# A grouped attention kernel whose Q rows stand in another order in three of eight chunks, and whose output is stored in an 8 by 8 pattern

## The chip, the cores and the metric

The kernel runs on one core of one Trainium2 chip. The metric is the device time in microseconds. Three runs of the kernel before took 341.83, 343.13 and 343.47 us; their median, 343.13 us, is the time before. Durations inside the kernel come from one profiled execution.

The core has five engines with a queue of instructions each: PE (TensorE, the matmuls), DVE (VectorE), ACT (ScalarE), POOL (GpSimd) and SP (SyncE, which here only issues DMAs). Sixteen DMA engines move the data between the memory of the chip and SBUF.

## The reference, cut to what matters

```python
B, Hq, Hkv, Sq, Sk, D = 16, 32, 8, 16, 2048, 128      # q, k, v in bfloat16
k = jnp.repeat(k, 4, axis=1); v = jnp.repeat(v, 4, axis=1)
scores = einsum("bhqd,bhkd->bhqk", q, k) * D ** -0.5
out = einsum("bhqk,bhkd->bhqd", softmax(scores, axis=-1), v)
```

Four query heads of 16 rows share one head of K and V. So each of the 16 x 8 = 128 K/V heads meets 64 rows of Q, which lie behind one another in memory. K and V are 67 MB each, Q and the output 2.1 MB each.

## The kernel before, in words

**Units.** A *pair* p (0 to 63) is two K/V heads, and so 128 rows of Q and of the output: the first 64 partitions belong to one head and the last 64 to the other. K is loaded for two pairs at once (32 loads of 2 MB, `Kn`, three slots), V for one pair (64 loads of 1 MB, `Vb`, seven slots; the last is cut into two DMAs), Q for a *chunk* of eight pairs (8 loads of 256 KB, `Qn`, two slots), and the output is stored pair by pair (64 stores of 32 KB from eight buffers `Osb`, 128 rows of 256 B each).

**Q.** A chunk c has 1024 rows. Its load (`load_q`) puts eight rows that follow one another into each partition: row 8a + j lies in partition a at place j. POOL (DVE for chunk 0) makes four masked copies in `Q4` (`lay_q`, L174). PE transposes them by matmuls with the identity (L278), four 128x128 tiles into one PSUM bank of 512 columns (a *stage*), and ACT evicts each stage to `QT` (L404). There are four such evictions in a chunk. In PSUM the columns stand as (j, a); the eviction turns them into (a, x, j), which is the order of the rows in memory: in steps over j, four elements at a time, it reads with a stride of 128 elements and writes 4 elements in a row. Columns of `QT` are the weights of the score matmuls, so their order is the order of the rows of scores, and of the partitions of the output.

**One pair.** DVE transposes K (two STREAM_TRANSPOSE for each score step, `kt`, L351). PE computes scores (L300 and L256). DVE takes them from PSUM, scaled and with the row's extreme (L373). ACT computes exp with the row sum (L413). PE transposes the weights (L312), ACT evicts them (L423), PE multiplies with V (PV, L330 for most pairs, L336 for each fourth and the last eight), and ACT divides by the row sum into `Osb` (norm, L436 and L440; for the last five pairs DVE does it, L394).

**Order.** The programs of PE and ACT are written out beforehand (`pe_prog`, `act_prog`): scores run two pairs ahead, PV four pairs behind (`PVLAG`), and the four parts of the next chunk's Q follow the pairs 2 to 5 of a chunk.

**SP's queue.** SP goes through steps t. In a step it issues, in this order: a Q load where t = 8c - 7; for even t the K load t/2, after a wait for its slot (L208); the V load of pair t - 6, after a wait for its slot (L216); and the store of pair t - 14, after a wait for its norm (L236). All DMAs go through one queue. At the end SP waits until all stores have landed. Before a buffer `Osb[p % 8]` is written again, ACT or DVE waits for the store of pair p - 8 by the count of its semaphore, which grows by 16 with each store.

Of the kernel before, what the change touches and what calls it, by code (L numbers as in the profile page):

```python
# [5 lines left out]
ACT = mybir.ActivationFunctionType  # L6
# [10 lines left out]
NO = 8  # L17
# [6 lines left out]
LASTV = ((0, 12), (12, 16))  # L24
NFAST = 8
NLATE = 5


def both_heads(p, NP):
# [3 lines left out]
def bass_standalone__gqa_softmax__sampling_kernel(  # L33
# [11 lines left out]
    NP = G // 2  # L45
# [21 lines left out]
    QT = [sb(f"QT{i}", [128, 2, 1024], F32) for i in range(2)]  # L67
# [28 lines left out]
    sem_ev = sem("sem_ev")  # L96
# [61 lines left out]
    last_q = {what[1:]: u for u, what in enumerate(stages) if what[0] == "Q"}  # L158
    last_p = {what[1:]: u for u, what in enumerate(stages) if what[0] == "P"}

    def stage_ap(u):
        return ST_ps[:, 512 * (u % NSTAGE):512 * (u % NSTAGE + 1)]

# [15 lines left out]
    with nc.Block() as block:  # L179
# [22 lines left out]
        @block.sync  # L202
        def _(sp):
            def load_k(n):
                s = n % NK
                if n >= NK:
                    sp.wait_ge(sem_kt, 4 * (n - NK) + 4)
                sp.dma_start(Kn[s][:, :], kf[n]).then_inc(sem_k[s], 16)  # L208

            def load_v(p):  # L210
                s = p % NV
                if p >= NV:
                    sp.wait_ge(sem_pv, p - NV + 1)
                if p < NP - 1:
                    dst = Vb[s][:, :, :, :].rearrange("a g j d -> a g (j d)")
                    sp.dma_start(dst, vf[:, 2 * p:2 * p + 2, :]).then_inc(sem_v[s], 16)  # L216
                    return
                for x, (lo, hi) in enumerate(LASTV):
                    dst = Vb[s][:, :, lo:hi, :].rearrange("a g j d -> a g (j d)")
                    src = vf[:, 2 * p:2 * p + 2, 128 * lo:128 * hi]  # L220
                    sp.dma_start(dst, src).then_inc(sem_vl[x], 16)

            def load_q(c):
                s = c % NQ
                if c >= NQ:
                    sp.wait_ge(sem_q4, 4 * (c - NQ + 1))
                src = qf[1024 * c:1024 * (c + 1), :].rearrange("(a j) d -> a j d", j=8)
                sp.dma_start(Qn[s][:, :, :], src).then_inc(sem_q[s], 16)

            def store(p):  # L230
                s = p % NO
                if p < NP - NLATE:
                    sp.wait_ge(sem_nm, p + 1)
                else:
                    sp.wait_ge(sem_nl, p - (NP - NLATE) + 1)
                sp.dma_start(of[128 * p:128 * (p + 1), :], Osb[s][:, :]).then_inc(sem_o[s], 16)  # L236

            for t in range(NP + SLAG + 1):
                for c in range(NQC):
                    if t == max(0, 8 * c - QLEAD):  # L240
                        load_q(c)
                if t < NP and t % 2 == 0:
                    load_k(t // 2)
                if 0 <= t - VLAG < NP:
                    load_v(t - VLAG)
                if 0 <= t - SLAG < NP:
                    store(t - SLAG)
            for s in range(NO):
                sp.wait_ge(sem_o[s], 16 * (NP // NO))

        @block.tensor
        def _(pe):
# [92 lines left out]
        @block.vector  # L345
        def _(dve):
            def kt(n, e):
                Q, x = divmod(n, 2)
                if x == 0:
                    dve.wait_ge(sem_k[Q % NK], 16 * (Q // NK + 1))  # L350
                dve.transpose(  # L351
                    KT[n % NKT][:, :].rearrange("p (t b g e a) -> p e g t b a", t=J // 4, b=2, g=4, e=2)[:, e],
                    Kn[Q % NK][:, :].bitcast(F32).rearrange(
                        "p (g x t e b c) -> p x e g t b c", g=4, x=2, e=2, b=2, c=32)[:, x, e],
                ).then_inc(sem_kt, 1)

            def recip(Q):
                dve.wait_ge(sem_exp, 2 * Q + 2)
                dve.reciprocal(rrec[:, 2 * Q:2 * Q + 2], rowsum[:, 2 * Q:2 * Q + 2]).then_inc(sem_rec, 1)  # L359

            dve.wait_ge(sem_id, 8)
            lay_q(dve, 0)
            for n in range(2):
                for e in range(2):
                    kt(n, e)
            for n in range(NP):
                Q, x = divmod(n, 2)
                dve.wait_ge(sem_s, n + 1)
                for y in range(2):
                    p = 2 * Q + y  # L370
                    if x == 0 and p >= NS:
                        dve.wait_ge(sem_exp, p - NS + 1)
                    dve.tensor_scalar(  # L373
                        Sneg[p % NS][:, 1024 * x:1024 * (x + 1)].rearrange("p (t a m) -> p t a m", t=4, m=8),
                        S_ps[:, 1024 * y:1024 * (y + 1)].rearrange("p (t m a) -> p t a m", t=4, m=8), -scale, None,
                        op0=ALU.mult, op1=ALU.min, accum_out=nhalf[:, x, p:p + 1],
                    ).then_inc(sem_max, 1)
                if x == 1:
                    dve.wait_ge(sem_max, 2 * n + 2)
                    pair = slice(2 * Q, 2 * Q + 2)  # L380
                    dve.tensor_tensor(nbias[:, pair], nhalf[:, 0, pair], nhalf[:, 1, pair], op=ALU.min).then_inc(sem_nb, 1)  # L381
                elif n >= 4:
                    recip(Q - 2)
                if n + 2 < NP:
                    for e in range(2):
                        kt(n + 2, e)
            recip(NQD - 2)
            for p in range(NP - NLATE, NP):
                if p == NP - 2:
                    recip(NQD - 1)  # L390
                dve.wait_ge(sem_rec, p // 2 + 1)
                dve.wait_ge(sem_o[p % NO], 16 * (p // NO))
                dve.wait_ge(sem_pv, p + 1)
                dve.tensor_scalar(Osb[p % NO][:, :], o_ap(p), rrec[:, p:p + 1], None, op0=ALU.mult).then_inc(sem_nl, 1)  # L394

        @block.scalar
        def _(act):
            for op in act_prog:
                if op[0] == "qe":
                    _, c, i, u = op  # L400
                    act.wait_ge(sem_st, u + 1)
                    if c >= 2 and i == 0:
                        act.wait_ge(sem_s, 8 * (c - 1))
                    act.activation(  # L404
                        QT[c % 2][:, i // 2, :].rearrange("p (a x j) -> p x a j", x=2, j=4)[:, i % 2],
                        stage_ap(u).rearrange("p (j a) -> p a j", j=4), ACT.Copy,
                    ).then_inc(sem_ev, 1)
                elif op[0] == "exp":
                    _, p = op
                    act.wait_ge(sem_nb, p // 2 + 1)  # L410
                    if p >= 2:
                        act.wait_ge(sem_st, last_p[p - 2, 1] + 1)
                    act.activation(  # L413
                        P[p % 2][:, :].bitcast(BF16),
                        Sneg[p % NS][:, :], ACT.Exp,
                        bias=nbias[:, p:p + 1], scale=-1.0, accum_out=rowsum[:, p:p + 1],
                    ).then_inc(sem_exp, 1)
                elif op[0] == "pe":
                    _, p, h, u = op
                    act.wait_ge(sem_st, u + 1)  # L420
                    if h == 0 and p >= NPT:
                        act.wait_ge(sem_pv, p - NPT + 1)
                    act.activation(  # L423
                        PT[p % NPT][:, 4 * h:4 * (h + 1), :].rearrange("p t q -> p (t q)"),
                        stage_ap(u), ACT.Copy,
                    ).then_inc(sem_ev, 1)
                else:
                    _, p = op
                    act.wait_ge(sem_pv, p + 1)
                    act.wait_ge(sem_rec, p // 2 + 1)  # L430
                    if p >= NO:
                        act.wait_ge(sem_o[p % NO], 16 * (p // NO))
                    if both_heads(p, NP):
                        for g in range(2):
                            rows = slice(64 * g, 64 * (g + 1))
                            ins = act.activation(Osb[p % NO][rows, :], O_ps[rows, 128 * g:128 * (g + 1)], ACT.Copy,  # L436
                                                 scale=rrec[rows, p:p + 1])
                        ins.then_inc(sem_nm, 1)
                        continue
                    act.activation(Osb[p % NO][:, :], o_ap(p), ACT.Copy,  # L440
                                   scale=rrec[:, p:p + 1]).then_inc(sem_nm, 1)
# [28 lines left out]
```

## Time and profile before

| what | value |
| --- | --- |
| median of three runs | 343.13 us (341.83 to 343.47) |
| span of the profiled execution | 340.7 us |
| PE busy, matmuls | 304.3 us (89%) |
| DVE busy | 304.8 us (89%) |
| ACT busy | 253.6 us (74%) |
| POOL busy | 81.3 us (24%) |
| moved by DMA | 138.87 MB, mean 408 GB/s |
| median time from issue to landing | K 15.3, V 16.6, Q 13.3, stores 16.1 us |

The page of the profile gives the span, from the first to the last instruction, and no other time of that execution. The difference to the runs (2.4 us to their median) holds what lies around the span and what executions differ by.

How to read the lines that follow: a group's line names the line of the code, the engine, the operation, what it writes and reads, the number of instructions, the busy time, the mean of one in ns, and the idle time before it with what ended it. In the rows of 40 slices a digit is the busy share of a slice in tenths. In a timeline, the first number is the start and the second the duration in us; a DMA issue on SP is as long as SP was held by it.

### The profile page before, as it was taken

The numbers are of one execution on the slowest core, as the hardware profiler recorded it, in microseconds if no ns is written. First come the engines' busy times: TensorE is split into PE (matmuls) and PEld (weight loads), VectorE is DVE, ScalarE is ACT, GpSimd is POOL, SyncE is SP. The second block draws the span as 40 slices with busy tenths as digits, with TensorE's granted clock in tenths as the row PEclk, the third lists the DMA queues.
The fourth block names the chain that finished last, engine by engine and source line by source line (L and its number), as shares of the span: only waits on it lengthen the run. The fifth ranks groups of instructions, "written<-read, shape, count | busy, mean of one in ns | idle before, by whom it ended". The sixth has DMA issues, their size and how long they took to land.

```text
span 340.7 us, 7084 instructions
## 1 busy us (share of the span) xinstructions
PE 304.3 (89%) x3040; PEld 182.4 (54%) x2528; DVE 304.8 (89%) x457; ACT 253.6 (74%) x390; POOL 81.3 (24%) x40
## 2 busy tenths in 40 slices
PE   3466798999899998999989999999989999899987
PEld 3012355555655664566555556556645665555556
DVE  1879998999989997999989999899979999899952
ACT  3025776789777888778867897778887788678875
POOL 2840007500092004900075000920039000000000
PEclk9759999999999999999999999999999999999999
DMA  7999999999999999999999999999999999999993
GB/s 294 443 415 420 425 415 414 411 419 422 424 423 410 415 419 424 416 420 407 419 426 423 419 405 417 421 428 415 412 418 416 426 418 423 408 419 415 410 407 121
DMA packets 32688, 138.87 MB, mean 408 GB/s; under 512 B 10896, under 2 KB 11152, under 8 KB 28560
## 3 DMA queue, kind: packets, MB, share of 16 engines
q1 hardware_dynamic: 32656, 138.42, 99.5%
q8 instruction: 22, 0.36, 0.4%
q14 instruction: 10, 0.08, 0.1%
HBM read 136.31 MB, written 2.10 MB: 406 GB/s over the span
## 4 chain that ended last, share of the span: by engine, by line
PE 55%; DVE 28%; ACT 9%; issue 5%; DMA 2%; ACTq 0%; SPq 0%; DVEq 0%
PE O_ps L330 17%; DVE Sneg L373 17%; PE S_ps L300 14%; PE S_ps L256 12%; DVE KT L351 11%; PE ST_ps L312 8%; ACT P L413 4%; ACT QT L404 2%; DMA Kn<-in_k_dram 2%; PE ST_ps L278 2%; ACT PT L423 2%; ACT O L436 1%; PE S_ps L336 1%; PE O_ps L336 1%; DVE rrec L359 0%
## 5 line engine op out<-in xcount | busy, mean ns | idle before, releaser
L373 DVE TENSOR_SCALAR_CACHE_REDUCE Sneg<-S_ps 128x1024 f32<-128x1024 f32 x128 | 150.7, 1213 | 19.1 <-PE S_ps L256 18.9
L351 DVE STREAM_TRANSPOSE KT<-Kn 128x1024 f32<-128x1024 f32 x128 | 150.8, 1217 | 3.9 <-DMA Kn<-in_k_dram 3.9
L413 ACT ACTIVATE P<-Sneg,nbias 128x2048 bf16<-128x2048 f32 x64 | 128.2, 2004 | 16.1 <-DVE nbias L381 15.1
L300 PE MATMUL S_ps<-KT,QT 64*128 64x512 bf16 x512 | 103.5, 394 | 24.1 <-DVE Sneg L373 12.8
L174 POOL TENSOR_SCALAR Q<-Qn,mask 128x1024 bf16<-128x1024 bf16 x28 | 79.1, 2843 | 181.1 <-PE ST_ps L278 174.6
L256 PE MATMUL S_ps<-KT,QT 64*128 64x512 bf16 x512 | 103.1, 392 | 0.0
L330 PEld LDWEIGHTS O_ps<-Vb,PT 128*128 128x128 bf16 x672 | 62.4, 98 | 34.7 <-issue 28.0
L330 PE MATMUL O_ps<-Vb,PT 128*128 128x256 bf16 x672 | 80.7, 273 | 0.0
L423 ACT ACTIVATE PT<-ST_ps 128x512 f32<-128x512 f32 x128 | 69.3, 595 | 13.1 <-PE ST_ps L312 12.1
L300 PEld LDWEIGHTS S_ps<-KT,QT 64*128 64x128 bf16 x512 | 27.4, 94 | 93.7 <-issue 72.4
L312 PE MATMUL ST_ps<-ident,P 128*128 128x128 f32 x512 | 67.6, 275 | 4.1 <-ACT P L413 4.1
L436 ACT ACTIVATE O<-O_ps,rrec 64x128 bf16<-64x128 f32 x84 | 30.4, 362 | 46.2 <-PE O_ps L330 45.7
L312 PEld LDWEIGHTS ST_ps<-ident,P 128*128 128x128 f32 x512 | 56.9, 141 | 10.3 <-ACT P L413 7.8
L278 PE MATMUL ST_ps<-ident,Q 128*128 128x128 f32 x128 | 20.4, 291 | 5.2 <-DVE Q L174 5.2
L404 ACT ACTIVATE QT<-ST_ps 128x512 f32<-128x512 f32 x32 | 19.3, 604 | 5.1 <-PE ST_ps L278 5.1
L336 PEld LDWEIGHTS O_ps<-Vb,PT 128*64 128x64 bf16 x576 | 16.7, 110 | 11.5 <-issue 11.5
L336 PE MATMUL O_ps<-Vb,PT 128*64 128x128 bf16 x576 | 19.5, 221 | 0.6 <-ACT O L440 0.6
L278 PEld LDWEIGHTS ST_ps<-ident,Q 128*128 128x128 f32 x128 | 16.4, 152 | 5.2 <-issue 5.2
L413 ACT ACTIVATION_READ_ACCUMULATOR P<-Sneg,nbias 128x1 f32 x64 | 12.2, 191 | 0.0
L373 DVE DVE_READ_ACCUMULATOR Sneg<-S_ps 128x1 f32 x128 | 10.6, 83 | 0.0
L440 ACT ACTIVATE O<-O_ps,rrec 128x128 bf16<-128x128 f32 x17 | 6.0, 351 | 2.2 <-PE O_ps L336 2.2
L381 DVE TENSOR_TENSOR nbias<-nhalf 128x2 f32<-128x2 f32 x32 | 5.1, 160 | 1.1
(19 smaller groups left out, 20.1 us busy)
## 6 DMA issues: line engine op xcount, KB each, us to landing
Kn<-in_k_dram SPq DMA_DIRECT2D x32, 2048.0 KB, 15.3
Vb<-in_v_dram SPq DMA_DIRECT2D x63, 1024.0 KB, 16.6
Qn<-in_q_dram SPq DMA_DIRECT2D x8, 256.0 KB, 13.3
out_dram<-O SPq DMA_DIRECT2D x64, 32.0 KB, 16.1
Vb<-in_v_dram SPq DMA_DIRECT2D x1, 768.0 KB, 12.0
Vb<-in_v_dram SPq DMA_DIRECT2D x1, 256.0 KB, 12.3
```

Source lines behind the costliest of these rows:

```text
L174: eng.tensor_scalar(Q4[:, :, :, r, :].rearrange("p j b x -> p (j b) x"), src, mask[:, r:r + 1], None, op0=ALU.mult,).then_inc(sem_q4, 1)
L256: return pe.add_instruction(mybir.InstMatmult(name=nc.get_next_instruction_name(), engine=mybir.EngineType.PE, ins=[pe.lower_ap(rhs), pe.l ...
L278: ins = pe.transpose(dst[:, 128 * j:128 * (j + 1)], src[:, 4 * x + j, b, :], ident4[:, :])
L300: ins = pe.matmul(s_ap, w, x, start=(acc == 0), stop=(acc == 3))
L312: ins = pe.transpose(dst[:, 128 * t:128 * (t + 1)], P[p % 2][:, 128 * x:128 * (x + 1)], ident4[:, :])
L330: ins = pe.matmul(O_ps[:, 0:256], pt[:, j // 2, j % 2, :], Vb[p % NV][:, :, j, :], start=(j == 0), stop=(j == J - 1),)
L336: ins = pe.matmul(o_ap(p)[64 * g:64 * (g + 1), :], pt[:, j // 2, j % 2, 64 * g:64 * (g + 1)], Vb[p % NV][:, g, j, :], start=(j == 0), stop ...
L351: dve.transpose(KT[n % NKT][:, :].rearrange("p (t b g e a) -> p e g t b a", t=J // 4, b=2, g=4, e=2)[:, e], Kn[Q % NK][:, :].bitcast(F32). ...
L373: dve.tensor_scalar(Sneg[p % NS][:, 1024 * x:1024 * (x + 1)].rearrange("p (t a m) -> p t a m", t=4, m=8), S_ps[:, 1024 * y:1024 * (y + 1)] ...
L413: act.activation(P[p % 2][:, :].bitcast(BF16), Sneg[p % NS][:, :], ACT.Exp, bias=nbias[:, p:p + 1], scale=-1.0, accum_out=rowsum[:, p:p + ...
L423: act.activation(PT[p % NPT][:, 4 * h:4 * (h + 1), :].rearrange("p t q -> p (t q)"), stage_ap(u), ACT.Copy,).then_inc(sem_ev, 1)
L436: ins = act.activation(Osb[p % NO][rows, :], O_ps[rows, 128 * g:128 * (g + 1)], ACT.Copy, scale=rrec[rows, p:p + 1])
```

## The change

`TURNED = (1, 3, 5)` names three chunks, 24 of the 64 pairs. In these chunks

- the eviction of Q writes the 64 rows of a head in the order (x, j, a) in place of (a, x, j): the row 8a + j of a head comes to the place 8j + a, in steps of eight rows. It reads eight neighbouring elements of PSUM at a time and writes 32 in a row.
- the rows of scores, of the weights and of O stand in that order too. Nothing else in the computation changes.
- a store is two DMAs, one for each half of 64 partitions, and the rows of the output are named by a pattern j, a: partition 8j + a goes to row 8a + j. Each adds 16 to the semaphore, 32 for the pair, and the waits for a buffer count accordingly (`stored`).

```diff
+TURNED = (1, 3, 5)
...
+    def stored(p):
+        return sum(32 if x // 8 in TURNED else 16 for x in range(p % NO, p + 1, NO))
...
-                sp.dma_start(of[128 * p:128 * (p + 1), :], Osb[s][:, :]).then_inc(sem_o[s], 16)
+                if p // 8 not in TURNED:
+                    sp.dma_start(of[128 * p:128 * (p + 1), :], Osb[s][:, :]).then_inc(sem_o[s], 16)
+                    return
+                for g in range(2):
+                    rows = of[128 * p + 64 * g:128 * p + 64 * (g + 1), :].rearrange("(a j) d -> j a d", j=8)
+                    sp.dma_start(rows, Osb[s][64 * g:64 * (g + 1), :]).then_inc(sem_o[s], 16)
...
-                dve.wait_ge(sem_o[p % NO], 16 * (p // NO))
+                dve.wait_ge(sem_o[p % NO], stored(p - NO))
...
-                    act.activation(
-                        QT[c % 2][:, i // 2, :].rearrange("p (a x j) -> p x a j", x=2, j=4)[:, i % 2],
-                        stage_ap(u).rearrange("p (j a) -> p a j", j=4), ACT.Copy,
-                    ).then_inc(sem_ev, 1)
+                    if c in TURNED:
+                        to = QT[c % 2][:, i // 2, :].rearrange("p (h x j a) -> p x h j a", x=2, j=4, a=8)[:, i % 2]
+                        turned = stage_ap(u).rearrange("p (j h a) -> p h j a", j=4, a=8)
+                    else:
+                        to = QT[c % 2][:, i // 2, :].rearrange("p (a x j) -> p x a j", x=2, j=4)[:, i % 2]
+                        turned = stage_ap(u).rearrange("p (j a) -> p a j", j=4)
+                    act.activation(to, turned, ACT.Copy).then_inc(sem_ev, 1)
```

The waits of ACT before a norm and of SP at the end are changed in the same way.

More of the change, by code (lines that the diff above doesn't have):

```diff
@@ L248, in _ @@
             for s in range(NO):
-                sp.wait_ge(sem_o[s], 16 * (NP // NO))
+                sp.wait_ge(sem_o[s], stored(NP - NO + s))
         @block.tensor
@@ L431, in _ @@
                     if p >= NO:
-                        act.wait_ge(sem_o[p % NO], 16 * (p // NO))
+                        act.wait_ge(sem_o[p % NO], stored(p - NO))
                     if both_heads(p, NP):
```

## The prediction

> **What bounds the kernel now.** I read the page first, then the instructions of the K loads, the queue of SP in order of time, and the end of PE.
>
> ```profile
> span 340.7 us, 7084 instructions
> ...
> DMA  7999999999999999999999999999999999999993
> DMA packets 32688, 138.87 MB, mean 408 GB/s; under 512 B 10896, under 2 KB 11152, under 8 KB 28560
> q1 hardware_dynamic: 32656, 138.42, 99.5%
> PE 55%; DVE 28%; ACT 9%; issue 5%; DMA 2%; ACTq 0%; SPq 0%; DVEq 0%
> L404 ACT ACTIVATE QT<-ST_ps 128x512 f32<-128x512 f32 x32 | 19.3, 604 | 5.1 <-PE ST_ps L278 5.1
> ```
>
> By the chain, PE and DVE set the end and the DMA has 2%. But the DMA engines are busy from the first slice to the last but one. Both are true: the loads arrive just in time. The next lines show how just. First the last K load in the view of its tile (window 295 to 297), then the DVE timeline at the transpose that reads it:
>
> ```profile
> L208 SPq DMA_DIRECT2D Kn<-in_k_dram x1: 1220/1220/1220, 295.8 to 295.8; - x1
> DMA to landing us min/median/max: 19.9/19.9/19.9
> ```
>
> ```profile
> 316.24 1.22 DVE L351 STREAM_TRANSPOSE KT<-Kn 128x1024 f32<-128x1024 f32 x1
> ```
>
> Issued at 295.76 us, landed 19.9 us later: 315.6. DVE came to it at 316.24. The spare time is 0.6 us. The same subtraction for earlier K loads gives 4.2 us (K25, wanted at 257.67), 2.6 (K27), 1.1 (K28), 2.3 (K29), 1.6 (K30): the loads fall behind, about 10.1 us for two pairs of heads where compute takes 9.4 to 10. V of the last pair lands at 336.0 and 336.8 us (issued 324.02 and 324.45, 12.0 and 12.3 us to landing), and PE reaches it at about 337.3 and 338.1: 1.3 us. The queue of SP shows the same from the other side:
>
> ```profile
> 186.04 0.47 SPq L236 DMA_DIRECT2D out_dram<-O  x1
> ...
> 297.51 6.55 SPq L236 DMA_DIRECT2D out_dram<-O  x1
> ```
>
> The same store takes 0.47 us to issue, and 6.55 us late in the run, where the queue is full and SP waits for room. So the kernel is bound by compute with 0.6 us to spare, and whatever the engines of the DMA have to do beyond that comes out at the end.
>
> One thing more, from the trace's records of the landings: each DMA lands in sixteen parts, one for each engine (169 DMAs, 169 x 16 = 2704 parts; with 64 x 128 = 8192 packets of store rows that makes the page's 10896 under 512 B). Early on the sixteen parts land within 0.6 us. At the end they do not: of the last V, six land between 331.9 and 332.8 us, four between 334.7 and 335.1, six between 335.6 and 336.8. Ten engines have been set back, by the fetches of instructions (22 packets of 16 KB, about 1.05 us each; late parts appear one after another behind them). A load is there when the latest engine is.
>
> **The change part by part.**
>
> *QT eviction (ACT L404).* 12 of 32 evictions get another pattern: 8 elements in a row are read and 32 in a row written, where 4 were written and each read was strided. The old pattern takes 604 ns with the strided read, and the plain 128x512 copy on L423 takes 595 (578 to 608). The pattern has no price for reading or writing in steps, so none is to be got back: 12 x 0.009 = 0.1 us at most in the mean, 12 x 0.026 = 0.3 us at the best case of L423. The third level is new for ACT; the three-level strided read by DVE on L373 takes 1213 ns for 1024 elements, no dearer per element than the plain 1217 of L351. Upper end 0.1 us each, 1.2 in all; I take 0. Four such evictions stand at the head of a chunk, where PE waited for QT 8.5 us in 7 waits (view of waits). But a gain there is worth nothing when K is late anyhow.
>
> *S, exp, PT, PV, norm.* The same instructions on the same addresses; the 64 rows of a head only stand in another order, and O comes out in that order. 0.
>
> *SP.* 24 stores become 48: 24 more issues at 0.47 us, 11.3 us of SP. SP waits 123.5 us for the slots of K alone (its view of waits), and in a round of two pairs (about 10 us) it issues some 2.1 us where the queue has room; 3.1 then. Hidden; were the cover gone, a K load would go out 1 us later per round, behind a backlog of 15 to 20 us, which changes its place in the queue and not its landing.
>
> *Waiting for the stores.* The wait for two halves (32 counts) ends with the second half. A buffer of O is written again 8 pairs later, some 39 us; the store of pair 48 lands at 318.4 us and its buffer is wanted at about 328.7. 10 us of cover; 0.
>
> *The DMA engines.* Here lies the price. A store of before has 128 rows in its outermost step, and each of sixteen engines gets 8 rows of 256 B. A half in the new pattern has the outermost step j, which counts 8, on the side of the output. If a DMA is dealt out along that step, there are eight pieces for sixteen engines, of 8 rows each; and if both halves are dealt from the same start, the same eight engines carry 16 rows for such a pair and the other eight none. I take this as likeliest: every DMA of the trace before has 128 as its outermost count and lands in 16 equal parts, which fits a split along that step. No row shows a count of 8, nor where the second half starts.
>
> By the Trainium skill (DMA: Bandwidth & Descriptors, in the section on why a DMA increments its semaphore by 16), the number of engines is the largest up to 16 that divides the outermost counts of both sides, and the lowest-numbered ones are used. By it, 64 and 8 give eight engines, the same for both halves, and the sum below stands as it is. No run here shows that yet.
>
> What 8 more rows and one more count cost an engine, 24 times:
> - lower end: the earliest part of a K load follows that of the load before by 10.00 us without stores between them (K7 and K6) and by 10.135 with two, in the middle of the run (landing records): 0.065 us a store. 24 x 0.065 = 1.6 us.
> - in the packet records a 256 B packet follows the last by 14.2 ns and the count takes 6: 8 x 14.2 + 6 = 0.12 us. 24 x 0.12 = 2.9 us.
> - upper end: the stores after the last V, with no load between, land 0.20 us apart. 24 x 0.20 = 4.8 us.
>
> I take 2.9: the small price of the first row comes from single stores that hide behind the slack of the loads next to them, and a double one has less of that; the last row has nothing around it. Of this the last K load bears all, since the last turned store (pair 47) is queued before it. 2.9 - 0.6 of spare time = 2.3 us, if a late engine is among the eight. Bounds: 1.6 - 0.6 = 1.0 and 4.8 - 0.6 = 4.2. At K28 about 19 of the 24 are through: 19 x 0.12 = 2.3 late against 1.1 to spare, less than at the last K, so the last K decides. V of the last pair is then 2.9 late against 1.3 + 2.3, no more wait.
>
> **Sum.** 340.7 + 2.3 = 343.0 us of span. The page has no time of its own beyond the span; the runs have a median of 343.13 (341.83 to 343.47), 2.4 above the span, which holds what lies around the span and the difference between executions. I carry the 2.3 over: **345.4 us**, its own range 344.1 to 347.3.
>
> **The rivals.**
>
> *All sixteen take part, no change.* If the halves are dealt by rows (64 into sixteen parts of 4) or the second half goes to the other eight, each engine moves the same rows and one count more: 24 x 9 ns = 0.2 us, within the 0.6. Time 343.1. For it: all the 169 DMAs now use sixteen. Against it: the count of 8. The Trainium skill has a sentence for this side too, in the rules for kernel authors of the same page: two transfers of partition halves serialize, since both spray across all 16 engines.
>
> *The late engines are relieved, not slower.* The eight that lose their rows could be late ones. Then 336.8 becomes 336.8 - 2.9 = 333.9 for them, and what counts is the late engines among the loaded eight: at least two of ten, at best those at 334.7 and 334.9. At 1.6 a pair of these comes at 336.5, earlier than 336.8. It decides in favour below 336.8 - 334.9 = 1.9 us of added load. The profiled execution waits for no load, so it would gain nothing; an execution that does (the median is 1.3 above the fastest run) could fall to 341.8. For it: ten of sixteen are late, so the spared half may well hold most. Against it: it needs the low price and the luckiest share.
>
> *Scattered rows cost more.* An engine writes 8 rows that stand 2 KB apart instead of 4 next to each other, twice. If such a row took as long as a 1024 B packet (46 ns in the records), a turned pair would cost 16 x 46 + 12 ns = 0.75 instead of 0.12: 24 x 0.63 = 15.1, less 0.6: 357.6 us. Against it: Q loads have a step too, and 2048 B take 84 ns, the rate of the long ones.
>
> **How the numbers follow.** Eight engines and a late one among them 0.60; sixteen 0.17; relieved 0.11; scattered 0.08; others 0.04. The range 342.5 to 348.0 takes in the forecast's bounds, the case of no change and part of the relief; outside lie the scattered case and the best of the relief. A measurement of this kernel tells some 0.5% (1.7 us) from no change. Slower by more is above 344.85: an added load above 2.3 us, which is 0.52 of my 0.60; with the scattered case (0.08) and the others (0.04, waits that I have not seen) 0.64. Faster by more, below 341.4, asks for more than the relief gives: 0.06. The rest is within 0.5%: 0.08 of the forecast, 0.17, and 0.05 of the relief, 0.30.
>
> **What will show it.** Right: packets in all stay 32688 (48 halves with 8 counts are 24 with 16; sixteen engines would give 33072); the mean DMA share stays near full while a DVE transpose waits for K near the end, by some 2 us, where now only the first does; L404 stays at 595 to 610 ns; waits for K's slots shrink on SP. Wrong: 33072 packets, or no wait on K late in the run, or 256 B packets that take longer than 18 ns.

## The result, and the profile after

The changed kernel takes 344.27 us (median of nine runs, 344.03 to 345.52), the kernel before 343.13 us (nine runs, 341.83 to 343.86). The ratio is 1.0043 with a 95% interval of 1.0027 to 1.0058: slower by 1.1 us, less than the 2.3 us that I forecast.

The profiled execution of the changed kernel took 344.03 us, of which its span is 341.9. First its page:

```profile
span 341.9 us, 7108 instructions
...
DMA packets 32688, 138.87 MB, mean 406 GB/s; under 512 B 10896, under 2 KB 11152, under 8 KB 28560
q1 hardware_dynamic: 32656, 138.42, 99.3%
...
PE 54%; DVE 24%; ACT 9%; DMA 8%; issue 5%; ACTq 0%; SPq 0%; DVEq 0%
...
L360 DVE STREAM_TRANSPOSE KT<-Kn 128x1024 f32<-128x1024 f32 x128 | 150.9, 1217 | 6.2 <-DMA Kn<-in_k_dram 6.2
...
L419 ACT ACTIVATE QT<-ST_ps 128x512 f32<-128x512 f32 x32 | 19.3, 603 | 5.3 <-PE ST_ps L287 5.3
```

Four readings. There are 24 DMAs more, and not one packet more: 48 half stores with eight counts each are as many as 24 with sixteen, so each half store is dealt to eight engines. The rule of the Trainium skill (DMA: Bandwidth & Descriptors, the section on why a DMA increments its semaphore by 16) gives eight for outermost counts of 64 and 8; the trace agrees, with 32688. The landing records say the same: the data of a half store land in eight parts, those of a whole store in sixteen (a half has a ninth record too, 0.4 us after its issue and long before the data). The eviction (L404 before, L419 now) takes 603 ns where it took 604. The share of the DMA in the chain went from 2% to 8%. And DVE waits 6.2 us for K, where it waited 3.9 us before, all of it then for the first load. The last two are no marks of the change: the page of e5_scatter16 below, a kernel that is no slower than the one before, has 8% and 6.2 us as well.

The timeline of DVE shows where the other waits are; the bracket at the end is the idle time before the line and what ended it:

```profile
285.57 2.37 DVE L360 STREAM_TRANSPOSE KT<-Kn 128x1024 f32<-128x1024 f32 x2 [0.68 <-DMA Kn<-in_k_dram]
...
306.76 2.37 DVE L360 STREAM_TRANSPOSE KT<-Kn 128x1024 f32<-128x1024 f32 x2 [1.07 <-DMA Kn<-in_k_dram]
...
317.14 2.37 DVE L360 STREAM_TRANSPOSE KT<-Kn 128x1024 f32<-128x1024 f32 x2 [0.92 <-DMA Kn<-in_k_dram]
```

These are K28, K30 and K31, the last. In the view of the tile, the last one was issued at 298.7 and landed 18.5 us later, at 317.1:

```profile
L212 SPq DMA_DIRECT2D Kn<-in_k_dram x1: 3831/3831/3831, 298.7 to 298.7; - x1
...
  DVE KT L360: 0.9, 1
...
DMA to landing us min/median/max: 18.5/18.5/18.5
```

It landed at 315.6 before, and DVE took it up at 316.24; now at 317.14, 0.9 us later. Of its sixteen parts the first lands 1.2 us earlier than before (309.86, before 311.04) and the last 1.5 us later: some engines have less to do, others more, as they must if both halves go to the same eight.

The rest of the 1.2 us between the spans is at the end of PE. PV of pair 61 took 1.35 us (the second line below, of the changed kernel) where it had taken 1.08 (the first, of the kernel before), while its V (332.6) and the following one (335.17) had landed:

```profile
334.27 1.08 PE L336 MATMUL S_ps<-Vb,PT 128*64 128x128 bf16 x32
...
335.19 1.35 PE L345 MATMUL S_ps<-Vb,PT 128*64 128x128 bf16 x32
```

The profile names nothing that it waited for, and no run was made for these 0.27 us.

The three late waits add up to 2.67 us, more than the 0.9. In this execution compute was ahead before them: K26 was taken up at 265.79, before the change at 267.06. It gave this lead up again in waits.

### The profile page after: what moved, and what is told of

It is laid out like the page before. It is cut to its first block, busy times and chain, and to the rows that moved or that the text cites. A ratio compares the mean times of both kernels' runs of the same rounds, so it can differ in the third digit from the quotient of the medians.

```text
span 341.9 us, 7108 instructions
## 1 busy us (share of the span) xinstructions
PE 304.3 (89%) x3040; PEld 183.1 (54%) x2528; DVE 305.0 (89%) x457; ACT 254.1 (74%) x390; POOL 81.4 (24%) x40
## 2 busy tenths in 40 slices
DMA packets 32688, 138.87 MB, mean 406 GB/s; under 512 B 10896, under 2 KB 11152, under 8 KB 28560
## 4 chain that ended last, share of the span: by engine, by line
PE 54%; DVE 24%; ACT 9%; DMA 8%; issue 5%; ACTq 0%; SPq 0%; DVEq 0%
PE O_ps L339 17%; DVE Sneg L382 14%; PE S_ps L309 13%; PE S_ps L265 12%; DVE KT L360 9%; PE ST_ps L321 8%; DMA Kn<-in_k_dram 8%; ACT P L425 4%; ACT QT L419 2%; PE ST_ps L287 2%; ACT PT L435 2%; ACT O L448 1%; PE S_ps L345 1%; PE O_ps L345 1%; DVE rrec L368 0%
## 5 line engine op out<-in xcount | busy, mean ns | idle before, releaser
L321 PE MATMUL ST_ps<-ident,P 128*128 128x128 f32 x512 | 68.4, 277 | 4.2 <-ACT P L425 4.1
L321 PEld LDWEIGHTS ST_ps<-ident,P 128*128 128x128 f32 x512 | 57.6, 142 | 10.7 <-ACT P L425 8.6
L419 ACT ACTIVATE QT<-ST_ps 128x512 f32<-128x512 f32 x32 | 19.3, 603 | 5.3 <-PE ST_ps L287 5.3
```

The source lines that it names most:

```text
L321: ins = pe.transpose(dst[:, 128 * t:128 * (t + 1)], P[p % 2][:, 128 * x:128 * (x + 1)], ident4[:, :])
```

## The experiments

Eleven kernels, each timed beside the kernel before on the same chip. The ratio is to that, with its 95% interval. The chips differ in the time of the kernel before, so ratios are compared, not times. Where Q and the stores are not turned together (e1, e2, e5, e7), the output rows of the turned chunks lie in another order; e6 leaves out the second half store of each turned pair, and e8 writes over the rows of other pairs.

| kernel | stores of the turned pairs | time, us | before, us | ratio |
| --- | --- | --- | --- | --- |
| changed kernel | two halves, 8 by 8, eight engines | 344.27 | 343.13 | 1.0043 (1.0027 to 1.0058) |
| e1_qt_only | plain | 343.09 | 342.94 | 1.0010 (0.9995 to 1.0024) |
| e2_store_only | two halves, 8 by 8 | 344.14 | 342.94 | 1.0030 (1.0015 to 1.0045) |
| e3_halves16 | two halves, plain | 342.98 | 342.94 | 1.0001 (0.9985 to 1.0017) |
| e4_all_turned | all 64 pairs | 349.22 | 342.94 | 1.0173 (1.0159 to 1.0188) |
| e5_scatter16 | two halves, 16 by 4 | 342.68 | 342.80 | 1.0000 (0.9988 to 1.0011) |
| e6_first_half | first half only | 342.24 | 342.80 | 0.9989 (0.9978 to 1.0000) |
| e7_near8 | two halves, 8 blocks of 8 near rows | 344.27 | 342.80 | 1.0041 (1.0029 to 1.0053) |
| e8_twice | plain, and a second time | 344.53 | 342.80 | 1.0053 (1.0040 to 1.0066) |
| e9_six | 48 pairs | 346.63 | 342.68 | 1.0124 (1.0108 to 1.0140) |
| e10_one | 8 pairs | 342.68 | 342.68 | 0.9997 (0.9983 to 1.0011) |
| e11_two | 16 pairs | 343.35 | 342.68 | 1.0029 (1.0015 to 1.0043) |

**The two parts apart.** First the eviction alone, then the store alone.

```diff
 # e1_qt_only, against the changed kernel
-                if p // 8 not in TURNED:
...
+                sp.dma_start(of[128 * p:128 * (p + 1), :], Osb[s][:, :]).then_inc(sem_o[s], 16)
```

> Q evicted in the new order in chunks 1, 3 and 5, but each pair stored by one plain DMA of 128 rows, so that the output rows of these chunks lie in the turned order. Engine theory (the price is the double rows on eight DMA engines): no price left, 343.1 us as before (342.6 to 343.6). Rival, eviction (the three-level pattern on ACT costs): 344.3, and L419 at more than 607 ns in twelve evictions.

```diff
 # e2_store_only, against the changed kernel
-                    if c in TURNED:
+                    if c < 0:
```

> Q evicted as before, but the pairs of chunks 1, 3 and 5 stored by two DMAs in the 8 by 8 pattern, so that the output rows of these chunks lie in the turned order. Engine theory: the whole price, 344.3 us (343.9 to 344.8), and the K loads 28 to 31 late as in the changed kernel. Rival, eviction: 343.1.

Measured: 343.09 and 344.14 us. The eviction costs nothing that could be told from noise (twelve of its 32 instructions have the new pattern, and all lie between 598 and 605 ns in e1). The store alone has the price. In the timeline of DVE of e2_store_only the last K load is late again, as in the changed kernel:

```profile
317.79 2.37 DVE L360 STREAM_TRANSPOSE KT<-Kn 128x1024 f32<-128x1024 f32 x2 [1.07 <-DMA Kn<-in_k_dram]
```

Of the rest of what I expected here, waits at K28 to K31, only this one came; the loads before it landed at 285.5, 295.8 and 306.2, just as late, but compute was later too in that execution.

**What of the store?** It is two DMAs and not one, its rows stand apart in memory, and it goes to eight engines. Three kernels take these apart. All have Q as before.

```diff
 # e3_halves16
-                    rows = of[128 * p + 64 * g:128 * p + 64 * (g + 1), :].rearrange("(a j) d -> j a d", j=8)
+                    rows = of[128 * p + 64 * g:128 * p + 64 * (g + 1), :]
 # e5_scatter16
+                    rows = of[128 * p + 64 * g:128 * p + 64 * (g + 1), :].rearrange("(a j) d -> j a d", j=16)
 # e7_near8
+                    rows = of[128 * p:128 * (p + 1), :].rearrange("(i g j) d -> g i j d", g=2, j=8)[g]
```

> Q as before; the pairs of chunks 1, 3 and 5 stored by two plain DMAs of 64 rows each, outermost count 64. Engine theory: sixteen engines with 4 rows each per half, 33072 packets, one count more per pair and engine (24 x 9 ns = 0.2 us): 343.2 us (342.7 to 343.7). Rival, number of DMAs (48 issues on SP instead of 24, or the packets of their counts, set the price): 344.3.

> Q as before; the pairs of chunks 1, 3 and 5 stored by two DMAs whose rows stand in a 16 by 4 pattern (j of 16 outermost, rows 16 apart inside), so that the output rows of these chunks lie in another order. Engine theory: 16 divides, sixteen engines with 4 scattered rows each, 33072 packets, 343.2 us (342.7 to 343.7). Rival, scattered rows (rows apart from each other in memory cost more): 344.3 or more.

> Q as before; the pairs of chunks 1, 3 and 5 stored by two DMAs of eight blocks of 8 rows that stand next to each other (2 KB), blocks 16 rows apart, outermost count 8; output rows of these chunks in another order. Engine theory: eight engines again, whether rows are near or apart, 32688 packets, 344.3 us (343.8 to 344.8). Rival, scattered rows: 343.1.

The page of e3_halves16 has 384 packets more than that of the changed kernel, and the page of e5_scatter16 has the same number. This is the line of e3_halves16:

```profile
DMA packets 33072, 138.87 MB, mean 408 GB/s; under 512 B 11280, under 2 KB 11536, under 8 KB 28944
```

and that of e7_near8 has this one:

```profile
DMA packets 32688, 138.87 MB, mean 406 GB/s; under 512 B 10896, under 2 KB 11152, under 8 KB 28560
```

So the times go by the number of engines. Two DMAs on sixteen engines cost nothing (342.98), nor do rows 16 apart on sixteen engines (342.68). Rows near each other on eight engines cost what the change costs (344.27). Of what was tried (outermost counts of 8, 16 and 64, rows near and apart), only the count of 8 changes the number of engines, and only that costs time. The rivals of the number of DMAs and of the scattered rows fall.

**Is it the load of the loaded engines, or that the load is uneven?** e6 leaves the eight engines the rows that they have before the change, and spares the others. e8 gives all sixteen the rows that the change gives to eight.

```diff
 # e6_first_half, against the changed kernel
-                for g in range(2):
+                for g in range(1):
 # e8_twice, plain stores, Q as before
+                for g in range(2 if p // 8 in TURNED else 1):
+                    at = p - 8 * g
+                    sp.dma_start(of[128 * at:128 * (at + 1), :], Osb[s][:, :]).then_inc(sem_o[s], 16)
```

> The changed kernel without the second half store of each turned pair (64 of 128 output rows of these pairs are left out). Engine theory: the eight engines carry 8 rows a pair as before the change, the other eight none: 343.1 us, or a little less if a late engine is among the spared (342.3 to 343.4). Rival, concentration (any DMA on eight engines only costs, by a queue held up or by uneven engines): about half the price, 343.7.

> Q as before, plain stores of 128 rows on sixteen engines; in chunks 1, 3 and 5 each pair is stored a second time, over the rows of the pair eight before it. All sixteen engines carry 8 rows and one count more for 24 pairs, as only eight do in the changed kernel. Engine theory: the latest engine decides, so the price is at least that of the changed kernel: 344.3 us (343.9 to 344.9). Rival, concentration (uneven engines are the price): 343.1 to 343.5.

342.24 us: uneven engines alone cost nothing. 344.53 us: evenly more is no cheaper than the change. In e8_twice DVE waits for four late K loads:

```profile
286.80 2.37 DVE L357 STREAM_TRANSPOSE KT<-Kn 128x1024 f32<-128x1024 f32 x2 [1.40 <-DMA Kn<-in_k_dram]
297.09 2.37 DVE L357 STREAM_TRANSPOSE KT<-Kn 128x1024 f32<-128x1024 f32 x2 [0.28 <-DMA Kn<-in_k_dram]
307.50 2.37 DVE L357 STREAM_TRANSPOSE KT<-Kn 128x1024 f32<-128x1024 f32 x2 [0.94 <-DMA Kn<-in_k_dram]
317.73 2.37 DVE L357 STREAM_TRANSPOSE KT<-Kn 128x1024 f32<-128x1024 f32 x2 [0.77 <-DMA Kn<-in_k_dram]
```

Such waits alone prove little: DVE also waits for the last K in the profiled executions of e1, e3 and e5, which have no price, and in e5 for two more. This is the last one of e5_scatter16:

```profile
315.86 2.37 DVE L360 STREAM_TRANSPOSE KT<-Kn 128x1024 f32<-128x1024 f32 x2 [0.65 <-DMA Kn<-in_k_dram]
```

What tells the kernels apart is when the last K lands: 315.8 here, 317.7 in e8.

e6 also tells something of the latest engine. Its loaded engines have the load of before, and its last K lands at 315.0 (issued 294.6, 20.4 to landing), where it lands between 315.6 and 315.8 in the kernel before, e1, e3 and e5. So the latest engines of those were, by this one execution, among the eight that e6 spares.

**The price of a pair.** All chunks turned:

```diff
-TURNED = (1, 3, 5)
+TURNED = (0, 1, 2, 3, 4, 5, 6, 7)
```

> All eight chunks turned, 128 half stores. Engine theory: 1.4 us late for 24 pairs (the last K lands 1.5 us later, the earliest engines differ by 1.1 to 1.2) is 0.055 to 0.06 us a pair; some 50 of 64 pairs are stored ahead of the last K and 55 ahead of the last V, so 2.9 to 3.2 us where the changed kernel has 1.4: 345.9 us (345.3 to 346.6). By the 0.12 us of the prediction: 24 more pairs at 0.12, 347.5 or more. Rivals with no link to the number of stores: 344.3.

349.22 us, 3.3 more than I expected. The landings gave a better price. A round is two pairs, with one K load. In the records of the changed kernel and of e4, the latest part of a K load follows that of the load before by some 10.33 us in many rounds with turned pairs (mostly 10.26 to 10.39), where it is 10.08 to 10.14 in rounds without: 0.2 us for the two pairs of a round, 0.10 a pair. In e8 most such rounds take 10.26 to 10.34 us on the earliest engine as well. On spared engines a round takes about 10.0, 0.07 less a pair. With 24 x 0.10 = 2.4 us the last K would have come 2.4 us later if the latest engine were a loaded one; it came 1.5 later. I took the missing 0.9 us for the distance at which the latest loaded engine stood ahead of the latest of all; the next runs bear this out only in part.

By that e4 has 50 x 0.10 - 0.9 = 4.1 us at the last K, and measured 4.6 (320.2 against 315.6). DVE took this K up 4.0 us later than before (320.23 against 316.24); the spans differ by 6.6. Of the 2.6 us that come behind it, 1.7 are at the very end, in the view of SP's instruction on line 245 (the half store) after 340 us:

```profile
L245 SPq DMA_DIRECT2D out_dram<-O x9: 593/606/606, 339.9 to 345.1; - x9
```

A half store of this pattern holds SP for 0.60 us where the queue is empty, a plain store 0.33. The last pairs are stored one behind the other after the last norm: in e4 3.7 us pass between the last norm and the end, before the change 1.95. The other 0.9 us are again at PV of pair 61, where PE stands still for 0.64 us after the fifth matmul:

```profile
339.28 0.97 PE L345 MATMUL S_ps<-Vb,PT 128*64 128x128 bf16 x27 [0.64 <-issue]
```

That is the place at which the changed kernel lost its 0.27 us. In the packet records a fetch of instructions (16 KB) starts 2.0 us before this PV in the changed kernel and 1.5 us before it in e4, and PE goes on 2.4 and 2.5 us after that start. In the other eleven profiles, which lose nothing there, the fetch starts 2.7 to 4.0 us before this PV. A PE that waits for its own instructions would fit that, but no run tests it.

**The price tested again, without the end.** Three doses:

```diff
 # e9_six; e10_one; e11_two
+TURNED = (0, 1, 2, 3, 4, 5)
+TURNED = (1,)
+TURNED = (1, 3)
```

> Chunks 0 to 5 turned, 48 pairs, all stored ahead of the last K and none at the very end. Theory as mended by the K landings (a turned pair costs the loaded engines 0.10 us, since the latest part of K comes 10.33 us after the last one where it is 10.13 without; the latest loaded engine was 0.9 us ahead of the latest of all): last K at 314.7 + 4.8 = 319.5 us, 3.3 behind the time at which DVE wants it, and V of pair 62 some 0.3 to 0.9 late: 343.0 + 3.8 = 346.8 us (346.2 to 347.3). Rival, the price grows with the count from the first pair on (1.14 us for 24): 345.3. With 0.12 a pair: 347.8.

> Chunk 1 alone turned, 8 pairs. Mended theory: last K at 314.7 + 0.8 = 315.5 us on the loaded engines, 315.0 on the others, both ahead of the want at 316.24: no change, 343.0 us (342.6 to 343.3). Rival, price from the first pair on: 343.4.

> Chunks 1 and 3 turned, 16 pairs. Mended theory: last K at 314.7 + 1.6 = 316.3 us, where DVE wants it: 343.1 us (342.8 to 343.5). Rival, price from the first pair on: 343.8.

48 pairs: 346.63 us against 346.8 expected by 0.10 a pair, and 345.3 and 347.8 by the others. Its last K was issued at 300.9 and landed 19.4 us later, 0.8 later than I worked out, and DVE waits for six late K loads, of which these are the last five:

```profile
267.10 2.37 DVE L360 STREAM_TRANSPOSE KT<-Kn 128x1024 f32<-128x1024 f32 x2 [0.81 <-DMA Kn<-in_k_dram]
277.44 2.37 DVE L360 STREAM_TRANSPOSE KT<-Kn 128x1024 f32<-128x1024 f32 x2 [0.89 <-DMA Kn<-in_k_dram]
287.78 2.37 DVE L360 STREAM_TRANSPOSE KT<-Kn 128x1024 f32<-128x1024 f32 x2 [0.88 <-DMA Kn<-in_k_dram]
309.31 2.37 DVE L360 STREAM_TRANSPOSE KT<-Kn 128x1024 f32<-128x1024 f32 x2 [1.77 <-DMA Kn<-in_k_dram]
320.32 2.37 DVE L360 STREAM_TRANSPOSE KT<-Kn 128x1024 f32<-128x1024 f32 x2 [1.54 <-DMA Kn<-in_k_dram]
```

That the time fits so well is in part luck: the last K came 0.8 us later than worked out, and the 0.3 to 0.9 us that I had added for V of pair 62 did not come (from the last K to the end it is 24.5 us, as in the kernel before).

Eight pairs: 342.68 us, no change, and no late wait for K; the last K lands at 315.5, as worked out, and DVE comes to it in the same moment (315.52), so that no reserve was left in this execution. Sixteen pairs: the last K lands at 316.35, as worked out too (316.3), but the time is 0.3% up, 0.15 to 0.43, between my 343.1 and the rival's 343.8. In its profiled execution compute was early and wanted this K at 315.5, so that DVE waited 0.91 us. The threshold is thus not one number: it lies where the loads meet compute, and compute comes by some tenths earlier or later from one execution to the next. The curve is flat up to 8 pairs, has begun to rise at 16, and rises by (346.63 - 342.68) - 1.14 = 2.8 us over the 24 pairs from 24 to 48, 0.12 a pair.

**All thirteen profiled executions beside each other.** The last column is the time from the moment at which DVE takes up the last K to the end of the span.

| kernel | double load | last K lands, us | DVE waited for it, us | from there to the end, us |
| --- | --- | --- | --- | --- |
| before | none | 315.6 | 0 (0.6 to spare) | 24.5 |
| e1, e3, e5 | none | 315.7, 315.7, 315.8 | 0.45, 0.20, 0.65 | 24.5 |
| e6_first_half | none, eight spared | 315.0 | 0.82 | 24.5 |
| e10_one | 8 pairs | 315.5 | 0 | 24.5 |
| e11_two | 16 pairs | 316.35 | 0.91 | 24.5 |
| changed kernel | 24 pairs | 317.1 | 0.92 | 24.8 |
| e2, e7 | 24 pairs | 317.8, 317.7 | 1.07, 1.23 | 24.5 |
| e8_twice | 24 pairs, all engines | 317.7 | 0.77 | 24.5 |
| e9_six | 48 pairs | 320.3 | 1.54 | 24.5 |
| e4_all_turned | about 50 pairs before it | 320.2 | 1.28 | 27.1 |

Two things follow. The end lies 24.5 us behind the last K everywhere but in the two executions that lost time at PV of pair 61 (and, in e4, at the last stores); and in every kernel but the one before and e10, DVE waits for that K. So its landing sets the span. And the distance of 0.9 us is not a property of the change: 315.6 plus 0.10 a pair, less the landing, leaves 0.9 in the changed kernel, in e10 and in e11, but 0.2 and 0.3 in e2 and e7, 0.1 in e9, 0.4 in e4, and 0.3 in e8, where all engines are loaded and there can be no such distance. Why it is there in some executions and not in others stays open.

## Why the prediction was right or wrong

- *The bound.* Right. Compute with a small reserve to the loads, and the last K load as the place where it is used up: the spans follow its landing, as the table shows. But the reserve is no fixed number: in e1, e3 and e5, whose stores put at most one count a pair more on an engine, there was none and DVE waited. The runs show it too: before they spread from 341.83 to 343.86, and eight of the nine of the changed kernel lie between 344.03 and 344.74, so that the fastest run moves by 2.2 us where the median moves by 1.14.
- *The mechanism.* Right: a half with an outermost count of 8 goes to eight engines (32688 packets), both halves to the same eight (the first part of the last K comes 1.2 us earlier and the last 1.5 later; and by the ratios of e6 and the changed kernel, 0.9989 and 1.0043, the second half alone costs 0.54%, 1.9 us, which it could not if it went to the spared ones).
- *QT eviction at 0.* Right: 603 ns, and e1.
- *SP at nothing.* Right for the change, by e3 (24 more issues, no change). The issue was priced at 0.47 us and takes 0.60; that matters only in e4, where the cover is gone at the end.
- *The price, 24 x 0.12 = 2.9 us.* Somewhat high by the landings: 0.10 a pair (2.4 us) by the rounds, and 0.08 to 0.09 (1.9 to 2.1 us) by the last K of e8, 317.7 against 315.6 to 315.8, where every engine has the double load. The slope of the medians from 24 to 48 pairs gives 0.12. So it lies between 0.08 and 0.12; of my three rows, the pitch of the packets (0.12) was the nearest, and the lower end, 0.065, was that of a single store between loads. (I priced a count at 6 ns here and at 9 in the rival of sixteen engines; over 24 pairs that is less than 0.1 us.)
- *"If a late engine is among the eight", and "of this the last K load bears all".* In the profiled changed kernel the last K came 1.5 us later, not 2.9: 0.5 for the price, if it is 0.10, and 0.9 for a loaded engine that was not the latest of all. I had treated the spare time of the latest engine as that of the loaded ones. But in e2 and e7, with the same load on eight engines, the last K came 2.1 to 2.2 us later, as in e8. So this step cost 0.9 us in some executions and 0.2 to 0.3 at most in others, and how much of the error of the median it made is not known.
- *Spare time 0.6 us.* Right in the pair of profiles: 1.5 - 0.6 = 0.9 us at the last K. It was a figure of one execution, as said above.
- *No more wait at V of the last pair.* Right; but PV of pair 61 lost 0.27 us in the profiled execution.
- *Sum.* 2.9 - 0.5 - 0.9 - 0.6 + 0.3 = 1.2 us of span, measured 1.2, for this pair of executions; in the medians 1.14 against my 2.3. The mechanism was right and the size was half; the range covered it. The error is shared by the price, the loaded engine that was not the latest, and a reserve that differs between executions, in shares that the runs do not settle.
- *The signs.* The packets (32688), the 603 ns of the eviction and the 18 ns of a 256 B packet came as written. Two signs came too, but prove nothing: a late wait for K stands in e1, e3 and e5 as well, and SP's waits for the slots of K shrank from 123.5 to 108.1 us, but to 88.7 in e5.
- *The chances.* I gave 0.64 to slower by over 0.5%, and 0.30 to a time within 0.5%. It came out at 0.43%, within the bound, and yet clear of no change: nine runs of each kernel tell less than the 0.5% that I had set.
- *The rivals.* "All sixteen take part" falls by the packets, and e3 shows that it would have cost nothing, as worked out. The sentence of the Trainium skill that I put beside it (DMA: Bandwidth & Descriptors, rules for kernel authors: halves spray across all sixteen) holds for e3, 33072 packets, and not for a half with the outer count 8. "The late engines are relieved" had something in it: in some executions the latest were among the spared, which made the price smaller and did not turn it. e6, where only this side acts, is faster by 0.11% (interval 0 to 0.22%). "Scattered rows" falls by e5 and e7.

## What to carry to other kernels

Look at the outermost count of both sides of a DMA before you rearrange the rows that it writes: here a pattern with 8 in front put the whole transfer on eight of sixteen engines, and as all engines were busy from end to end, the loads behind it waited for the most loaded one. Such a price begins only when the reserve between landing and use is gone. Take that reserve from more than one execution: it was 0.6 us in the profile that I had and nothing in three others. And choose a sign that only the change can give: late waits for K stood in kernels without a price, while the landing of the last K told them apart. A few doses of the same edit (8, 16, 24, 48 pairs) show threshold and slope better than one comparison.

## What the runs showed that I had not expected

A row of 256 B costs more in a double run than in a single one: 0.065 us for a store of eight rows and a count between loads, 0.08 to 0.12 for eight more behind them, 0.20 where stores follow each other alone. The engines that were spared gained 0.07 us a pair. And the pattern has a price on SP too: a half store takes 0.59 to 0.61 us to issue in an empty queue with eight by eight rows or with eight blocks of near rows; plain halves were issued in as little as 0.48 us, and those of 16 by 4 in 0.54.
